# Turning the second unit of each edge turn by DMA in the first column group of a windowed-attention backward kernel

## The chip, the cores and the metric

The kernel runs on one core of a Trainium2 chip. The metric is the device time of one execution in microseconds (us); lower is better. TensorE is PE in the profile, with its weight loads as PEld; VectorE is DVE, ScalarE is ACT, GpSimd is POOL, SyncE is SP. SP computes nothing here: it issues DMAs, in order, and waits in order.

## The reference, cut to what matters

A layer mixes sliding-window attention `a` and a gated feed-forward block `b` by a sigmoid gate `g`; the kernel returns the output and the gradients of all inputs and weights.

```python
qkv = (x @ wqkv).reshape(B, S, 3, H, Dh)             # S=2048, D=512, H=32, Dh=16
scores = einsum("bhqd,bhkd->bhqk", q, k) * Dh**-0.5
mask = (i - j >= 0) & (i - j < 256)                  # a window of 256 keys
p = softmax(where(mask, scores, -1e9));  a = (p @ v) @ wo
gate = x @ W_gate;  up = x @ W_up
b = (relu(gate) * up) @ W_down
g = sigmoid((x * gate_w).sum(-1));  out = g * a + (1 - g) * b
# and the vector-Jacobian product of out with grad_out, for x, wqkv, wo, W_gate, W_up, W_down, gate_w
```

## The kernel before, in words

There are three stages. The feed-forward stage, with its gradients, runs to about 257 us of the profiled span, the attention stage from there to about 713 us, and the last stage, which sums `out` and `dx`, to the end.

The attention stage works on four column groups `c` of 128 columns (8 heads each) and, within a group, on sixteen query blocks of 128 rows. The window lets a query block `q` see the key blocks `q`, `q-1` and `q-2`. The work is cut into *turns*: 46 in each column group, six for every two query blocks. A turn has two *units* (`x` = 0 and 1), each of two heads and up to two (query, key) blocks. Turns 0, 1, 3 and 4 of the six are pair turns (the blocks on and next to the diagonal). Turns 2 and 5 are *edge* turns: their blocks are `(k, k-2)`, where the window ends.

What happens to one turn, over the turns that follow it:

- `products` (L667): PE computes the scores S of this turn and, beside them, the products D of the turn before (`dO` times V). S and D have one PSUM buffer each.
- `front` (L700): ACT takes the exponential of S into the tile `PP`, for both units in one instruction. Edge turns use a tile of two buffers of their own, pair turns one of four; either way a buffer comes round again after six turns.
- `mask` (L710): POOL zeroes what lies outside the window. In an edge turn this is one instruction over the whole tile.
- `gradp` (L717), one turn later: DVE multiplies `PP` by D into the second half of `PP`.
- `flip`: the products for `dK` and `dV` need `PP` turned, with its rows on the other axis. Where `u.dma` is set, SP issues one DMA transpose (L763) right behind `gradp`, one turn after the unit's own. Where it isn't, PE turns eight 128x128 blocks (L771) two turns after the unit's own, into a PSUM tile that DVE or ACT then copies out (L74, L72; `share` picks the engine by a planner's running sum of costs). In the kernel before, of a turn with two blocks unit 0 goes by DMA and unit 1 by PE, except in the first two query blocks of group 0 and the last two of group 3, where all goes by PE.
- `rowsum` (L734, L736): PE sums over `PP`; POOL makes `rq` and others of it (L790 to L805).
- `cd_piece` (L492, L495): PE multiplies the turned `PP` by `rq`. A piece waits for its query block's sums plus three turns (`closed[...] + 3 <= turn`), which puts a turned edge unit's first use at least seven turns behind the unit's own.

The whole order is written out by a loop over `turn` under a manual schedule, so each engine has its instructions in a fixed order. Into the turns it also puts the projections of the next group (L146, L172: a DMA transpose of query and `dO` rows on SP, once in twelve turns), the stores of finished rows (`spill`, L506 on SP, 512 KB each), loads of turned weights (L523 on SP), and in groups 1 to 3 the weight gradients of the group before (L600, L603), whose inputs are loaded at L573.

The lines that decide how a unit is turned:

```python
u.edge = blocks[-1][1] == blocks[-1][0] - 2
u.dma = x == 0 and len(blocks) == 2 and (c > 0 or q > 0) and (c < DC - 1 or q < NT - 2)
u.turn = u.at + (1 if u.dma else 2)
```

Of the kernel before, what the change touches and what calls it, by code (L numbers as in the profile page):

```python
# [22 lines left out]
def kernel(  # L23
# [31 lines left out]
    NT = S // P  # L55
    DC = D // P
# [410 lines left out]
    if True:  # L467
# [166 lines left out]
        for c in range(DC):  # L634
            def pair_of(q):
                return [(q, q), (q + 1, q)]

            def edges_of(r):
                return [(k, k - 2) for k in (r, r + 1) if 2 <= k < NT]

            for q in range(0, NT, 2):
                if q + 2 < NT:
                    its = ((pair_of(q), 0), (pair_of(q), 2), (edges_of(q + 1), 0), (pair_of(q + 1), 2), (pair_of(q + 1), 0),
                           (edges_of(q + 2), 2))
                else:
                    its = ((pair_of(q), 0), (pair_of(q), 2), ([(q + 1, q + 1), (q + 1, q - 1)], 0), ([(q + 1, q + 1)], 2))
                for k, (blocks, g) in enumerate(its):
                    two = []
                    for x in range(2):
                        u = Unit()  # L650
                        u.c, u.q, u.g, u.x, u.blocks, u.nb, u.at = c, q + k // 3, g + x, x, blocks, len(blocks), len(turns_)
                        u.edge = blocks[-1][1] == blocks[-1][0] - 2
                        u.dma = x == 0 and len(blocks) == 2 and (c > 0 or q > 0) and (c < DC - 1 or q < NT - 2)
                        u.turn = u.at + (1 if u.dma else 2)
                        two.append(u)
                    turns_.append(two)
# [218 lines left out]
        with tc.manual_schedule():  # L875
# [49 lines left out]
            while turn < NI + 3 or ev or cdq or bg or sums:  # L925
# [9 lines left out]
                if us and (turn == 0 or turns_[turn - 1][0].q != us[0].q):  # L935
                    c, j = us[0].c, us[0].q
# [215 lines left out]
```

## Time and profile before

| | us |
|---|---|
| median of 3 runs | 911.15 (909.12 to 911.76) |
| the profiled execution | 905.92 |
| span in its profile | 904.2 |
| granted clock, mean over the span | 0.992 |
| first column group, first L700 to first L700 of the next group | 258.0 to 361.0 |
| groups 1 and 2, in the same way | 114.1, 115.1 |

The profiled execution took 1.7 us more than its span, and lies 5.2 us below the median of the timed runs. Times within the span are counted from its start. A busy share is the time in which an engine had an instruction, not the time in which it could not have taken another; SP's busy time is not counted on the page and is read from its timeline.

### The profile page before, as it was taken

The page shows a single profiled execution, that of the slowest core. Times are in us where ns is not written, and L with a number is a line of the kernel's source. Part 1 is how long each engine was busy: PE and PEld are TensorE (multiplying, and loading weights), DVE is VectorE, ACT ScalarE, POOL GpSimd, SP SyncE. Part 2 cuts the span into 40 slices and gives each one's busy share as a digit, 9 for nine tenths or more (in the row PEclk, how much of TensorE's full clock was granted, in tenths as well). Part 3 has the DMA queues.
Part 4 walks back from the last instruction along what each step waited for, and adds up shares of the span by engine and source line. Part 5 has one row for each costly group of instructions (what it writes and reads, how often), then busy time and mean ns, then how long its engine had stood idle before and what let it go on. Part 6 is the DMA issues. An engine that isn't in the chain of part 4 may idle for free. (4 is left out here: it accounts for less than half of the span.)

```text
span 904.2 us, 29627 instructions
## 1 busy us (share of the span) xinstructions
PE 865.2 (96%) x12569; PEld 563.4 (62%) x12569; DVE 492.8 (55%) x754; ACT 389.9 (43%) x565; POOL 474.5 (52%) x883
## 2 busy tenths in 40 slices
PE   7999999999988999999999999999899999999998
PEld 4566555565657777777777767777577744444443
DVE  4543322233247888878778777788677322322322
ACT  5522222223247676666557655667464311111111
POOL 2544444454327777976668766687566512222221
PEclk9999999999989999999999999999899999999999
DMA  9989899988726999999978999999999996777750
GB/s 282 210 182 228 214 209 201 225 202 199 191 56 96 149 148 170 146 152 217 181 113 140 132 238 161 135 164 173 219 178 216 248 278 155 187 196 193 195 124 27
DMA packets 444334, 161.25 MB, mean 178 GB/s; under 512 B 362696, under 2 KB 441896, under 8 KB 444200
## 3 DMA queue, kind: packets, MB, share of 16 engines
q1 hardware_dynamic: 418520, 133.13, 81.7%
q10 hardware_dynamic: 23856, 20.98, 8.2%
q0 software_dynamic: 1824, 5.25, 1.7%
q8 instruction: 98, 1.61, 0.7%
q14 instruction: 36, 0.29, 0.1%
HBM read 38.44 MB, written 38.41 MB: 85 GB/s over the span
## 5 line engine op out<-in xcount | busy, mean ns | idle before, releaser
L717 DVE TENSOR_TENSOR PP<-PP,D 128x1024 bf16<-128x1024 bf16 (+1 forms) x184 | 219.5, 1193 | 69.4 <-POOL PP L710 24.9
L700 ACT ACTIVATE PP<-S 128x1024 bf16<-128x1024 f32 (+1 forms) x184 | 185.2, 1006 | 96.3 <-PE D L667 48.2
L710 POOL TENSOR_SCALAR_AFFINE_SELECT PP<-PP 128x512 bf16<-128x512 bf16 (+1 forms) x188 | 143.5, 764 | 108.8 <-ACT PP L700 93.4
L74 DVE COPY p<-pt 128x1024 bf16<-128x1024 bf16 x167 | 114.3, 684 | 16.5 <-PE pt L771 16.3
L771 PE MATMUL pt<-ident,PP 128*128 128x128 bf16 x1536 | 117.9, 221 | 1.7 <-DVE p L74 0.9
L350 POOL TENSOR_TENSOR hT<-rg,upm 128x512 bf16<-128x512 bf16 x44 | 52.4, 1192 | 126.1 <-DVE upm L348 105.4
L734 PE MATMUL BA<-KV,PP 128*128 128x33 bf16 x1440 | 106.6, 180 | 6.1 <-ACT BAs L72 6.1
L383 PE MATMUL wps<-dgu_r,x_r 128*128 128x256 bf16 x704 | 105.6, 272 | 3.7 <-DVE wst L74 3.4
L734 PEld LDWEIGHTS <-PP 128*128 128x128 bf16 x1440 | 85.6, 96 | 31.2 <-issue 11.2
L736 PE MATMUL BA<-KV,PP 128*128 128x17 bf16 x1440 | 102.2, 170 | 0.3 <-issue 0.3
L492 PE MATMUL CD<-rq,p 128*128 128x32 bf16 x1440 | 95.0, 176 | 0.0
L495 PE MATMUL CD<-rq,p 128*128 128x16 bf16 x1440 | 93.8, 169 | 1.1 <-issue 1.1
L736 PEld LDWEIGHTS <-PP 128*128 128x128 bf16 x1440 | 84.7, 96 | 13.5 <-issue 8.6
L383 PEld LDWEIGHTS <-x_r 128*128 128x128 bf16 x704 | 68.8, 98 | 35.7 <-issue 5.4
L771 PEld LDWEIGHTS <-PP 128*128 128x128 bf16 x1536 | 89.5, 98 | 2.0 <-issue 2.0
L667 PE MATMUL S<-zT,K 32*128 32x128 bf16 (+3 forms) x1056 | 78.4, 241 | 5.4 <-ACT PP L700 2.7
L495 PEld LDWEIGHTS <-p 128*128 128x128 bf16 x1440 | 80.6, 96 | 1.5 <-issue 1.2
L492 PEld LDWEIGHTS <-p 128*128 128x128 bf16 x1440 | 80.8, 96 | 0.3
L667 PE MATMUL D<-zT,V 32*128 32x128 bf16 (+3 forms) x1056 | 73.3, 239 | 4.1 <-DVE PP L717 3.6
L1072 ACT COPY a_sb<-aps 128x512 f32<-128x512 f32 x16 | 9.4, 586 | 145.9 <-issue 133.0
L348 DVE SCALAR_TENSOR_TENSOR upm<-rg,ups 128x512 bf16<-128x512 bf16 x44 | 30.2, 686 | 68.5 <-PE ups L336 43.8
L385 PE MATMUL dps<-db_r,h_r 128*128 128x512 bf16 x176 | 66.7, 379 | 0.0
(144 smaller groups left out, 1471.4 us busy)
## 6 DMA issues: line engine op xcount, KB each, us to landing
dqkvo_d<-rows_st SPq DMA_DIRECT2D x14, 512.0 KB, 4.7
hT_d<-hT ACTq DMA_DIRECT2D x44, 128.0 KB, 2.5
dgT_d<-dgu ACTq DMA_DIRECT2D x44, 128.0 KB, 2.9
duT_d<-dgu ACTq DMA_DIRECT2D x44, 128.0 KB, 2.8
duT_g<-duT_d SPq DMA_DIRECT2D x8, 640.0 KB, 5.3
dgT_g<-dgT_d SPq DMA_DIRECT2D x7, 640.0 KB, 8.0
gt<-hT_d SPq DMA_DIRECT2D x7, 640.0 KB, 5.8
dar<-da_d SPq DMA_DIRECT2D x16, 256.0 KB, 4.6
```

The costliest lines, as they stand in the source:

```text
L74: nc.vector.tensor_copy(out, in_)
L383: nc.tensor.matmul(acc["w"][:, c, :], lhsT=x_r[:, t, c * P:(c + 1) * P], rhs=k.dgu_r[:, :, i, :], start=(go_ and c % 2 == 0), stop=no_, sk ...
L385: nc.tensor.matmul(acc["d"][:], lhsT=k.h_r[:, i, :], rhs=db_r[:, t, :], start=go_, stop=no_)
L492: nc.tensor.matmul(cd[0][:, h, :], lhsT=p2[:, 0, pr, :], rhs=rq[:, h, 0:2 * Dh], start=cd[1], stop=True, skip_group_check=True)
L495: nc.tensor.matmul(cd[0][:, h, 0:Dh], lhsT=p2[:, 1, pr, :], rhs=rq[:, h, 2 * Dh:3 * Dh], start=False, stop=True, skip_group_check=True)
L667: nc.tensor.matmul(dst, lhsT=proj[(u.c, kb // TPG)][nm + ("", "1")[par]][rows[par], (kb % TPG) * P:(kb % TPG + 1) * P], rhs=proj[(u.c, qb ...
L700: nc.scalar.activation(two[:].rearrange("p x a b q -> p x a (b q)")[:, :, 0, 0:n], flat(us[0].S[:], n), ACT.Exp)
L710: nc.gpsimd.affine_select(out=out, in_=out, compare_op=ALU.is_ge, fill=0.0, base=0 if up else -1, pattern=[[0, 2], [0, b1 - b0], [1 if up ...
L717: nc.vector.tensor_tensor(out=v(1), in0=v(0), in1=flat(vs[0].D[:], n), op=ALU.mult)
L734: nc.tensor.matmul(BA[:, h, 0:33], lhsT=u.PP[:, 0, 2 * i + pr, :], rhs=kv[:, kb % TPG, h, 1:34], start=(first and pr == 0), stop=True, ski ...
L736: nc.tensor.matmul(BA[:, h, 33:50], lhsT=u.PP[:, 1, 2 * i + pr, :], rhs=kv[:, kb % TPG, h, 0:17], start=False, stop=True, skip_group_check ...
L771: nc.tensor.transpose(pt[:, a, b if u.nb == 2 else 2 * u.x + b, :], u.PP[:, a, b, :], ident[:])
```

## The change

In column group 0, unit 1 of an edge turn with two blocks now also has `u.dma` set. So its `flip` is moved from two turns behind the unit to one turn behind it, and issues a DMA transpose on SP, directly behind that of unit 0, in the place of eight PE transposes and a copy out of PSUM. Thirteen units are concerned: two edge turns for each two query blocks from block 2 to block 13, and one for the last two. Nothing is changed for pair turns, for query blocks 0 and 1, or for the groups 1 to 3. As there are fewer copies to share out, `share` gives a few others to another engine: on the whole DVE has eight copies of turned units and two of `KV` fewer, ACT five copies of turned units fewer and two of `KV` more.

```diff
                         u.edge = blocks[-1][1] == blocks[-1][0] - 2
-                        u.dma = x == 0 and len(blocks) == 2 and (c > 0 or q > 0) and (c < DC - 1 or q < NT - 2)
+                        u.dma = (x == 0 or c == 0 and u.edge) and len(blocks) == 2 and (c > 0 or q > 0) and (c < DC - 1 or q < NT - 2)
                         u.turn = u.at + (1 if u.dma else 2)
```

## The prediction

> **What bounds the stage.** I read the windows first, cut to the stretch of group 0 in which turns go by DMA, then the groups of instructions of that stretch, then the timelines of PE, DVE and SP.
>
> ```profile
> 277.00:361.00 84.00, 81.11 (x2030) 64.10 (x2028) 73.77 (x106) 59.99 (x78) 66.88 (x150) 1.00 1.02 150
> ```
> ```profile
> L717 DVE TENSOR_TENSOR PP<-PP,D 128x1024 bf16<-128x1024 bf16 x39 | 47.2, 1211 | 8.4 <-POOL PP L710 7.5
> ...
> L771 PE MATMUL pt<-ident,PP 128*128 128x128 bf16 x312 | 23.7, 218 | 0.0
> L74 DVE COPY p<-pt 128x1024 bf16<-128x1024 bf16 x33 | 22.6, 684 | 0.5 <-PE pt L771 0.3
> ```
>
> The columns of the window are its length, then the busy time of PE, PEld, DVE, ACT and POOL, the clock, the DMA share and GB/s. PE is busy for 81.1 of 84 us and DVE for 73.8, at full clock. The turns repeat: three of them (two pair, one edge) take about 6.5 us (the L700 at 317.44, 318.94, 321.26 and 323.93 begin one such round). PE's timeline there is closed to within a tenth of a us at the scores of a turn. So PE bounds the stage, with DVE just behind it. SP's timeline shows the third resource:
>
> ```profile
> 336.83 3.45 SPq L763 DMA_TRANSPOSE p<-PP  x2
> 340.33 1.96 SPq L172 DMA_TRANSPOSE rows<-zT  x1
> 342.39 1.25 SPq L523 DMA_TRANSPOSE p<-in_A_wqkv_dram  x1
> 343.73 2.69 SPq L763 DMA_TRANSPOSE p<-PP  x2
> 346.48 1.72 SPq L523 DMA_TRANSPOSE p<-in_A_wqkv_dram  x1
> 348.28 9.68 SPq L763 DMA_TRANSPOSE p<-PP  x6
> ```
>
> These are issues with hardly a gap: for 21 us SP was behind, in the kernel before already.
>
> **What is taken off PE, DVE and ACT.** Each of the 13 units loses eight transposes:
>
> ```profile
> 322.35 0.46 PEld L771 LDWEIGHTS <-PP 128*128 128x128 bf16 x8
> 322.77 0.10 PEld L146 LDWEIGHTS <-p 128*128 128x128 bf16 x1
> ```
>
> The next work begins 0.42 to 0.44 us behind the first of them, so PE loses 13 x 0.44 = 5.7 us. DVE loses 8 copies of 0.684 and two of KV of 0.53, together 6.5 us; ACT loses 5 of 1.01 and gains two of 0.59, together 3.9 us off. Not all of the 5.7 would show. The flip removed stands in the third turn of a round. There DVE's L717 runs from 321.83 to 323.00, and the next products need D free. They began at 323.35, so a turn without the flip could start them at 323.0: 0.35 us gained. 13 x 0.35 = 4.6 us is the gain if nothing else is late; the ends are 0 (where the odd half of K or V stands ahead of L717 on DVE, as at 328.35) and 5.7.
>
> **What is added on SP.** 13 transposes, each directly behind its unit 0's. They wait for the same L717, so this wait is nothing new; what is new is SP's time:
>
> ```profile
> L763 SPq DMA_TRANSPOSE p<-PP x39: 1231/1302/2273, 277.3 to 361.3; - x39
> ...
> DMA to landing us min/median/max: 3.0/4.2/5.8
> ```
>
> An issue takes 1.23 us when SP is idle. With a queue it takes more: from 338.81 to 357.96 twelve transposes follow each other in 19.15 us, 1.60 each. Issues of 1.3 alternate with some of about 2.0. The long ones (340.33, 346.48, 351.03, 355.90) fall together with packets of the instruction queue:
>
> ```profile
> q8 instruction: 15, 0.25, 1.1%
> ```
>
> Fifteen of these, one in some 5.4 us, of 0.9 to 1.3 us each; during one, hardly a packet of a transpose is moved. Now the sum for SP, from the first round that is changed (issue at 282.30) to the end of group 0's last issue (362.70), 80.4 us. Before: 37 of L763, 4 of L172, 2 of L523, 43 transposes, and two stores (L506, 0.38 and 1.50 us). At 1.60 that is 68.8 + 1.9 = 70.7 us: it fits. After: 56 transposes, 89.6 + 1.9 = 91.5 us. It doesn't fit, by 11.1 us, even if the rest ran no faster than before. In a round of two query blocks (13.05 us) that is 8.5 transposes, 13.6 us, where 6.5 took 10.4.
>
> **Who waits.** A transpose reads `PP`, and L700 writes that buffer again six turns later; in the compiled order L700 waits for a DMA semaphore as well as for DVE and PE, in edge turns of the changed kernel for two. How late may SP be? An edge turn of before:
>
> ```profile
> 317.44 1.02 ACT L700 ACTIVATE PP<-S 128x1024 bf16<-128x1024 f32 x1
> ...
> 330.44 1.03 ACT L700 ACTIVATE PP<-S 128x1024 bf16<-128x1024 f32 x1
> ```
>
> Its transpose was issued at 320.90, with no lag, and landed 3.84 later, at 324.74; the buffer was wanted at 330.44. So 5.7 us were left. Over group 0 the sum of lag and margin is mostly 4.5 to 5.7; I take 5.0. In the busy stretch above, where lag was up to 3.7 us, only 1.1 of it was left: before, nothing waited, but it was near. Once it is used up, ACT waits in L700, with the copies of BA, K, V and zT (L72, L88) queued behind it, and PE for S at the next L667. The first use of a turned unit, seven turns on, comes later than this and so isn't what binds.
>
> **The sum.** 11.1 us too much SP work, less 5.0 that lag may take up, less about 1 that the first turns of group 1 give back (four transposes in five turns, with gaps of 2.0 and 2.8 us on SP): 5 us later than before at the end of the stage. The 4.6 us won on PE isn't subtracted: it only makes SP's queue begin to bind earlier. The chain behind the stage is PE's, and so 5 us go to the end. On the profile's own 905.9 that is 910.9; on the median, 5.2 higher, 911.15 + 5.0 = 916.1. I choose 1.60 because it is measured in this stage, with this traffic, at the first place where SP is behind. The other rows: 1.23 to 1.30 between instruction packets below, and above it this one of group 1, behind four loads of 256 KB:
>
> ```profile
> 376.83 11.09 SPq L763 DMA_TRANSPOSE p<-PP  x6
> ```
>
> which is 1.85 each.
>
> A figure from elsewhere would give another answer. The Trainium skill, in "DMA: Bandwidth & Descriptors", section "Latency and other measured facts", has an effective 261 GB/s for a DMA transpose: 256 KB in 1.0 us (an estimate from it), 58 us of work in the 80.4, and nothing would be late. The trace doesn't agree: 262 KB in 1.60 us is 164 GB/s. Against the change speaks a rule of the Trainium skill, in "VectorE: DVE Perf Modes", section "Rules for kernel authors": 128x128 on TensorE where PSUM will do, by DMA otherwise; it gives no price, and the trace has none for it but the queue above.
>
> **Rivals.**
>
> *SP is hidden, the kernel is faster.* If a queue were served at 1.33 us (1.29 and a gap, as between instruction packets), the work would be 56 x 1.33 + 1.9 = 76.4 us, in a stretch of 80.4 - 4.6 = 75.8; lag takes up the 0.6 that is over. Then 4.6 us are won: 911.15 - 4.6 = 906.6, at best 905.4. For it: two of three issues do take 1.3, and no L700 waits for a DMA before. Against it: the instruction packets come with PE's work and don't go away. The change turns from loss to gain where the SP work is (80.4 + 6.0 - 1.9) / 56 = 1.51 us each. Chance 0.23.
>
> *It comes out even.* From 343.73 to 351.03, five transposes take 7.30 us, 1.46 each; nine to 357.96 take 1.58. Between, at 1.52, 85.1 + 1.9 - 80.4 - 6.0 = 0.6 us: 911.8. Chance 0.20.
>
> *The queue does more harm than its own length.* At 1.72, between the two measured ends of a full queue, 96.3 + 1.9 - 80.4 - 6.0 = 11.8 us, 923: lag that is carried into group 1 meets its loads (L573) and stores, where 8 us to landing were seen. For it: the stores' transfers slow their neighbours (2.11 and 1.59 us at 310). Chance 0.12.
>
> That the change doesn't do what it says is ruled out: in the compiled order SP has 13 pairs of L763, and PE 104 transposes less.
>
> **Numbers.** The forecast (915 to 919) has 0.45, the harm case 0.12, even 0.20, faster 0.23. A run of this kernel can tell about 0.3% (2.7 us) from no change. That gives 0.23 faster, 0.20 same, 0.57 slower. The range runs from the faster case, nearly at its best, to just below the harm case's middle: 906.0 to 922.0. The likelier sign's own range is 914 to 923.
>
> **What would show it.** Right: in SP's timeline from about 300 on no gaps between issues, at 1.5 to 1.7 us each; in the waits, ACT's L700 on a DMA `p<-PP`, which before never shows, for 5 to 10 us in all, most of it past 335, where the stores and L523 come; PE's share in 277 to 361 below 0.93; group 0 at 106 to 109 us instead of 102.9, groups 1 and 2 at their 114 and 115. Wrong: SP keeping gaps of half a us in most rounds, no DMA in L700's waits, and rounds of 12.4 us instead of 13.05; then the cost per transpose is what failed. If L700 waits but the stage is no longer, the 5 us of margin were too few. Wrong in another way: if PE waits at L492 for a landing, or if the loss stands in groups 1 to 3.

## The result and the profile after

The changed kernel takes 917.6 us (median of 14 runs, 910.32 to 924.89), the kernel before, run between them, 910.99 (14 runs, 907.69 to 916.74). The ratio is 1.0075, with a 95% interval of 1.0049 to 1.0101: slower by 6.6 us, where 5.0 were forecast. A second measurement (run `after_again`, below) gives 1.0084. The first profile of the changed kernel fell on an execution in a slower state (924.89 us), so the lines below are from `after_again`, whose profiled execution took 916.87 us with a span of 915.2.

The window over the part of group 0 that the prediction read first (length, then busy time of PE, PEld, DVE, ACT and POOL, granted clock, DMA share, GB/s):

```profile
277.00:361.00 84.00, 75.85 (x1800) 57.14 (x1800) 65.22 (x91) 52.82 (x69) 62.35 (x140) 0.90 1.11 165
```

Every engine has got emptier: PE from 81.1 us to 75.9, DVE from 73.8 to 65.2. Only the DMA share went up, from 1.02 to 1.11. The granted clock fell from 1.00 to 0.90.

The groups of instructions of this stretch (window 277 to 369; busy time and mean ns, then idle time ahead and what ended it):

```profile
L717 DVE TENSOR_TENSOR PP<-PP,D 128x1024 bf16<-128x1024 bf16 x39 | 47.4, 1216 | 17.2 <-POOL PP L710 10.9 <-PE D L667 4.4 <-PE S L667 0.7
L700 ACT ACTIVATE PP<-S 128x1024 bf16<-128x1024 f32 (+1 forms) x40 | 40.5, 1012 | 26.7 <-PE D L667 12.4 <-DMA p<-PP 8.5 <-PE S L667 3.7
L771 PE MATMUL pt<-ident,PP 128*128 128x128 bf16 x224 | 18.5, 231 | 0.0
L74 DVE COPY p<-pt 128x1024 bf16<-128x1024 bf16 x26 | 17.8, 683 | 0.2
```

L717 costs what it cost, but now stands idle for 17.2 us where it was 8.4. L700 has a releaser that it didn't have before, `DMA p<-PP`: the transpose that still reads the buffer which L700 wants to write. SP's timeline (start, duration, issues):

```profile
291.09 22.23 SPq L763 DMA_TRANSPOSE p<-PP  x14
...
320.56 22.57 SPq L763 DMA_TRANSPOSE p<-PP  x14
...
343.86 3.57 SPq L763 DMA_TRANSPOSE p<-PP  x2
347.48 1.95 SPq L172 DMA_TRANSPOSE rows<-zT  x1
349.52 1.25 SPq L523 DMA_TRANSPOSE p<-in_A_wqkv_dram  x1
350.87 4.93 SPq L763 DMA_TRANSPOSE p<-PP  x3
355.85 1.29 SPq L523 DMA_TRANSPOSE p<-in_A_wqkv_dram  x1
357.24 12.60 SPq L763 DMA_TRANSPOSE p<-PP  x9
```

Fourteen issues in 22.23 us are 1.59 each, fourteen in 22.57 are 1.61. The longest gap between two issues from 283.25 to 377.67 us is 0.42 us: SP works through the whole of the changed part without a break.

### The profile page after: what moved, and what is told of

It is laid out like the page before. It is cut to its first block, busy times and chain, and to the rows that moved or that the text cites. A ratio compares the mean times of both kernels' runs of the same rounds, so it can differ in the third digit from the quotient of the medians.

```text
span 923.2 us, 29309 instructions
## 1 busy us (share of the span) xinstructions
PE 857.5 (93%) x12335; PEld 562.8 (61%) x12465; DVE 488.4 (53%) x744; ACT 386.2 (42%) x562; POOL 474.2 (51%) x883
## 3 DMA queue, kind: packets, MB, share of 16 engines
q8 instruction: 97, 1.59, 0.8%
## 5 line engine op out<-in xcount | busy, mean ns | idle before, releaser
L717 DVE TENSOR_TENSOR PP<-PP,D 128x1024 bf16<-128x1024 bf16 (+1 forms) x184 | 219.7, 1194 | 83.4 <-POOL PP L710 28.2
L700 ACT ACTIVATE PP<-S 128x1024 bf16<-128x1024 f32 (+1 forms) x184 | 185.1, 1006 | 119.4 <-PE D L667 57.0
L74 DVE COPY p<-pt 128x1024 bf16<-128x1024 bf16 x159 | 108.9, 685 | 15.3 <-PE pt L771 14.9
L771 PE MATMUL pt<-ident,PP 128*128 128x128 bf16 x1432 | 113.0, 225 | 1.0 <-DVE p L74 0.9
L495 PE MATMUL CD<-rq,p 128*128 128x16 bf16 x1440 | 94.1, 170 | 1.9 <-issue 1.9
L492 PE MATMUL CD<-rq,p 128*128 128x32 bf16 x1440 | 95.5, 177 | 0.3 <-DMA p<-PP 0.3
L667 PE MATMUL S<-zT,K 32*128 32x128 bf16 (+3 forms) x1056 | 80.5, 245 | 12.7 <-ACT PP L700 7.7
L495 PEld LDWEIGHTS <-p 128*128 128x128 bf16 x1440 | 81.0, 96 | 2.3 <-issue 2.0
L492 PEld LDWEIGHTS <-p 128*128 128x128 bf16 x1440 | 81.2, 96 | 0.7 <-DMA p<-PP 0.4
L667 PEld LDWEIGHTS <-K 16*128 16x128 bf16 (+1 forms) x1056 | 35.3, 94 | 51.4 <-issue 44.0
```

What stands on the lines that cost most here:

```text
L74: nc.vector.tensor_copy(out, in_)
L492: nc.tensor.matmul(cd[0][:, h, :], lhsT=p2[:, 0, pr, :], rhs=rq[:, h, 0:2 * Dh], start=cd[1], stop=True, skip_group_check=True)
L495: nc.tensor.matmul(cd[0][:, h, 0:Dh], lhsT=p2[:, 1, pr, :], rhs=rq[:, h, 2 * Dh:3 * Dh], start=False, stop=True, skip_group_check=True)
L667: nc.tensor.matmul(dst, lhsT=proj[(u.c, kb // TPG)][nm + ("", "1")[par]][rows[par], (kb % TPG) * P:(kb % TPG + 1) * P], rhs=proj[(u.c, qb ...
L700: nc.scalar.activation(two[:].rearrange("p x a b q -> p x a (b q)")[:, :, 0, 0:n], flat(us[0].S[:], n), ACT.Exp)
L717: nc.vector.tensor_tensor(out=v(1), in0=v(0), in1=flat(vs[0].D[:], n), op=ALU.mult)
```

## The experiments

All ratios are to the kernel before, measured on the same chip in the same session, with 95% intervals. Diffs are against the changed kernel unless they say "before".

The theory: the DMA transposes are served one after the other; with thirteen more the queue is longer than the stage, and `PP` buffers come free too late. The first rival says that the queue is harmless and something else about the thirteen units costs the time. The second says that PE's relief is real and only partly covered by the queue's loss, so that without it the loss would be 11 to 12 us. A third says that the time goes in stretches at half clock.

**The changed kernel once more** (`after_again`, no edit).

> The changed kernel once more, for a profile at full clock. Queue theory: the transposes of group 0 stand in one queue on SP, served at about 1.6 us each; once its lag has used up the six turns after which a PP buffer comes round, L700 waits. Then group 0 is 5 to 9 us longer than before, SP has no gaps from about 285 to 375, L700 waits for p<-PP by 5 to 12 us, and groups 1 and 2 are at 114 to 115. Total 5 to 8 us over before. Clock rival: the loss comes from stretches at half clock that follow pauses of PE. Then a profile at full clock shows group 0 no longer than 104 us.

Measured: 918.78 us, 1.0084 (1.0052 to 1.0116). The profile confirms the queue, but it isn't at full clock (0.979 over the span), so it doesn't decide against the clock. Nor do the timed runs: their median granted clock is 0.978, that of the kernel before in the same session 0.989, which over 916 us is some 10 us of full clock lost.

**The DMA without the relief** (`e_both`, from before). The thirteen units are turned on PE as before, and a DMA transpose of the same data goes into a tile that nobody reads.

```diff
+u.twice = c == 0 and u.edge and x == 1 and len(blocks) == 2 and q > 0
...
+elif v.twice:
+    spare = gwp.tile([P, 2, D], BF, tag="dar", bufs=4, name="spare")[:].rearrange("p a (b q) -> p (a b) q", q=P)
+    nc.sync.dma_start_transpose(out=spare, in_=v.PP.rearrange("p a b q -> p (a b) q"))
```

> The 13 units are turned on PE as before, and a DMA transpose of each is issued as well, into a spare tile that nobody reads; SP has the work of the changed kernel, PE, DVE and ACT that of before. Queue theory: PE's relief is worth nothing while the queue binds, so the time is that of the changed kernel within 1.5 us (5 to 8 us over before). Rival, a plain sum of the work taken off PE and a fixed price of each DMA: the 4.6 us of PE's relief are lost on top, 11 to 12 us over before.

Measured: 917.88 us, 1.0074 (1.0042 to 1.0105), the same as the changed kernel. In the waits of ACT (us in all, times, longest) the same exponential stands as L701:

```profile
ACT PP L701 <- DMA spare<-PP: 6.7, 2, 3.7
ACT PP L701 <- DMA p<-PP: 3.9, 2, 2.3
```

So the added DMAs by themselves bring a loss of this size, and the rival's 11 to 12 us are out. On balance, taking 104 transposes off PE and 8 copies off DVE is worth nothing as long as these DMAs are there. Whether that is because the queue alone sets the time is not shown: the median granted clock of these runs is 0.987, near that of the kernel before (0.989), where the changed kernel has 0.978. So `e_both` loses its 6.5 us with PE at almost the old clock, and the changed kernel with less work on PE at a lower clock; the relief may be lost to the clock as well as to the queue (see `e_fill`).

**The relief without the DMA** (`e_skip`, from before). The thirteen units are not turned at all; their products are made with unit 0's turned data in their place, so the output is not the reference's.

```diff
+u.skip = c == 0 and u.edge and x == 1 and len(blocks) == 2 and q > 0
-p2 = wides[u.at][:, u.x if u.nb == 2 else 0, :, :, :]
+p2 = wides[u.at][:, u.x if u.nb == 2 and not u.skip else 0, :, :, :]
+if u.skip:
+    return
```

> The 13 units are not turned at all (the output lacks their part of the key and value gradients: unit 0's turned data stand in for unit 1's); SP has the work of before, PE, DVE and ACT that of the changed kernel. Queue theory and the first part of the sum: 4.6 us faster than before (0 to 5.7), 0.995 of it. If PE's relief is worth nothing even without the queue, the same as before.

Measured: 907.28 us, 0.9957 (0.9936 to 0.9978), 4.1 us faster than before, and no exponential waits for a DMA. That is what the relief would bring if the DMA were free. Its one profile is of its slowest run (910.88 us) and has half clock too: three stretches between 275.5 and 313.0, 20.4 us in all, without a wait for a DMA, and a group 0 of 105.0 us. So not every half clock comes from the queue.

**Seven units instead of thirteen** (`e_k2`): of each two query blocks only the first edge turn.

```diff
-(x == 0 or c == 0 and u.edge)
+(x == 0 or c == 0 and u.edge and k == 2)
```

> Only the first edge turn of each six is changed, 7 units instead of 13. Queue theory: 50 transposes of 1.6 us and 1.9 of stores are 81.9 us in 80.4, and lag can take up 5, so hardly anything waits; 7 x 0.35 = 2.4 us of PE's relief are won, less about 1 for the bunch at the weight loads: 0 to 2.4 us faster than before. Rival, a fixed price of each transpose (6.6 us / 13 = 0.5 us): 3.5 us slower than before.

Measured: 909.83 us, 0.9984 (0.9963 to 1.0005). Seven of the thirteen transposes do not cost half the loss but none of it. The fixed price, 3.5 us slower, is outside the interval; a threshold fits. In the profile L700 still waited for a DMA in three turns, 3.5 us in all (here and below in the window 277 to 385, where the changed kernel has 10.8).

**Both units in one DMA** (`e_one`): the number of transposes is that of before, the bytes are those of the changed kernel.

```diff
+if vs and all(v.dma for v in vs):
+    for v in vs:
+        place(v)
+    nc.sync.dma_start_transpose(out=wides[vs[0].at][:].rearrange("p x a b q -> p (x a b) q"),
+                                in_=vs[0].two[:].rearrange("p x a b q -> p (x a b) q"))
```

> As the changed kernel, but the two units of such an edge turn are turned by one DMA transpose of 512 KB instead of two of 256 KB. If the queue's price goes by bytes (blocks that the DMA engines turn), one of these takes some 3.2 us of SP and the time stays at 5 to 8 us over before. If it goes by issue, 13 issues fall away, SP's work is that of before, and the time is that of the version that doesn't turn these units: about 4 us faster than before.

Measured: 916.29 us, 1.0037 (1.0015 to 1.0058). The large ones, by the view of that line (minimum, median and maximum ns):

```profile
L972 SPq DMA_TRANSPOSE p<-PP x13: 1844/2968/3229, 284.2 to 370.9; - x13
```

In this one profile (of an execution of 922.62 us) a transpose of 512 KB takes 2.97 us at the median, nearly twice the 1.6 of one with 256 KB. So the price goes mostly with the bytes; a fixed price per transpose would have made the kernel some 4 us faster than before. Thirteen of 2.97 us are 38.6 us of SP where twenty-six of 1.6 are 41.6. The loss is 3.4 us by the ratio instead of 6.6 to 7.4, but the intervals overlap, so that a saving is likely and not shown; L700 still waits for a DMA, 7.9 us in three turns.

**More `PP` buffers** (`e_ring`): in group 0 edge turns have four buffers instead of two and pair turns six instead of four; the added ones lie in a store buffer (`rows_st`) that isn't used yet.

```diff
+own, more = (2, 2) if edge else (4, 2)
+if us[0].c == 0:
...
+    i = ring.get(edge, 0)
+    ring[edge] = (i + 1) % (own + more)
+if i >= own:
+    k0 = (i - own + (0 if edge else 2)) * 16 * P
+    two = ring["tile"][:, k0:k0 + 16 * P].rearrange("p (x a b q) -> p x a b q", x=2, a=2, b=4)
```

> As the changed kernel, but in group 0 edge turns have four PP buffers instead of two and pair turns six instead of four (the added ones lie in the second rows_st buffer, which group 0 doesn't need): a buffer comes round after 12 and 9 turns instead of 6. Queue theory: L700's wait for p<-PP, 10.8 us in the changed kernel, goes to below 3 us in group 0; part of it comes back as PE waiting at L492 for a landing (first use is seven turns on, and a lag of 10 us with 4.5 to landing comes to that), and as lag that group 1 starts with. 0 to 5 us over before, so 2 to 6 us better than the changed kernel. If L700's wait were not what costs, the time stays at that of the changed kernel.

Measured: 919.62 us, 1.0073 (1.0047 to 1.0098): no better, which the theory as it stood did not expect. The waits of this kernel, window 277 to 385:

```profile
POOL rq L804 <- DMA rows<-zT: 5.3, 3, 4.7
PEld L492 <- DMA p<-ring: 2.1, 2, 1.5
PE CD L492 <- DMA p<-ring: 1.9, 2, 1.4
```

The exponential's wait on `p<-PP` is gone from group 0, but the time isn't. The turned rows (the transpose of L172) stand in the same queue and come late in their turn, as do the turned units for PE itself. The longest of these waits, 4.7 us of POOL, holds up the mask behind it, DVE's product behind the mask, and PE for 4.63 us up to 354.21. Here the queue found another waiter when the first was given room.

**Two loads moved out of the stage** (`e_late`): the two L523 transposes of `wqkv` at turns around 345 us are put into group 1.

```diff
-plan = {3: turns("wqkv", A_wqkv, 0, 4, "p0"), 7: turns("wqkv", A_wqkv, 4, 8, "p1"),
+plan = {7: turns("wqkv", A_wqkv, 0, 4, "p0") + turns("wqkv", A_wqkv, 4, 8, "p1"),
```

> As the changed kernel, but the two turned loads of wqkv (L523) that stand in group 0 at the queue's worst place are issued in group 1 instead. Queue theory: 2 x 1.6 = 3.2 us less SP work in group 0, and as L700 waits there, 3 us less of its waits: 2 to 5 us over before. If the loss were a fixed price of each of the 13 transposes, nothing changes: 5 to 8 us over before.

Measured: 915.93 us, 1.0042 (1.0017 to 1.0067). Two transposes fewer, 3.2 us of queue, and the loss is 3.7 us instead of 6.6 to 7.4; the intervals overlap, so this is a hint in the expected direction. L700's waits for a DMA fell only from 10.8 to 9.3 us, in five turns, where 3 us less were expected. The same edit made to the kernel before (`b_late`) is its control:

> The kernel before with only the two turned loads of wqkv moved from group 0 to group 1: a control for the other two. Queue theory: before, nothing waits for the queue in group 0, so the same as before within 0.2%. If group 0's bunch did cost before, 1 to 2 us faster.

Measured: 911.75 us, 1.0001 (0.9975 to 1.0026). In the kernel before, moving the loads is worth nothing that the measurement can tell.

**Four units** (`e_q4`): only query blocks 2 to 5, long before the stores and the loads.

```diff
-(x == 0 or c == 0 and u.edge)
+(x == 0 or c == 0 and u.edge and q < 6)
```

> Only the edge turns of the first two rounds (query blocks 2 to 5) are changed, 4 units, where SP still had gaps of about 1 us in each turn. Queue theory: no L700 waits for a DMA before 320 us of the span, lag there stays under 4 us, and 4 x 0.35 = 1.4 us are won: 0 to 2 us faster than before. A fixed price of 0.5 us for each: 2 us slower.

Measured: 910.68 us, 0.9980 (0.9963 to 0.9997), with no wait of L700 for a DMA. It has the lowest ratio of the versions that compute everything: 1.6 to 1.8 us better than the kernel before, which is hardly more than the measurement can tell, and its interval overlaps that of `e_k2`.

**Both ways to shorten the queue** (`e_late_k2`): seven units, and the two loads moved.

> Both reliefs of the queue together: the first edge turn of each six alone is changed (7 units), and the two turned loads of wqkv are issued in group 1. Queue theory: 48 transposes of 1.6 us and 1.9 are 78.7 us in 80.4, no bunch is left, lag stays under 4 us, L700 waits for no p<-PP in group 0, and all of 7 x 0.35 = 2.4 us is won: 2 to 3 us faster than before. A fixed price of each transpose: 3.5 us slower.

Measured: 911.36 us, 0.9994 (0.9971 to 1.0017). No L700 waited for a DMA in the profile, and yet the 2 to 3 us did not come. Why is open; the interval reaches from 2.6 us faster to 1.5 us slower.

**Work put into PE's pause** (`e_fill`): 22 matmuls without use, some 2.4 us, in turn 39, into a PSUM half that nobody reads.

```diff
+if turn == 39:
+    for _ in range(22):
+        nc.tensor.matmul(CDs["spare"], lhsT=ident[:], rhs=x_r[:, 0, 0:2 * P], start=False, stop=True, skip_group_check=True)
```

> As the changed kernel, but in turn 39 PE gets 22 matmuls into an unused half of a PSUM bank (about 2.4 us that nobody reads), just where it stood still for 2.5 us in the changed kernel's profile because L700 waited for a landing; there 10.2 us at half the granted clock followed. If that pause brings the half clock, and it costs: no half clock at 350 to 362, and 2 to 4 us better than the changed kernel. If the queue alone sets the time, within 1.5 us of the changed kernel either way. If PE doesn't stand still there, 2.4 us worse.

What it is for shows in three windows of `after_again` around the wait at 349 us:

```profile
345.00:349.00 4.00, 4.00 (x86) 2.79 (x85) 3.02 (x4) 1.51 (x2) 3.47 (x7) 1.00 1.36 182
349.00:351.50 2.50, 0.19 (x4) 0.05 (x3) 1.25 (x4) 1.51 (x3) 0.42 (x1) 1.00 0.87 188
351.50:362.00 10.50, 9.91 (x192) 6.99 (x192) 6.24 (x9) 5.67 (x9) 6.63 (x18) 0.51 1.18 183
```

PE stands for 2.31 us, from 349.13 to 351.45, and over the next 10.5 us its granted clock is 0.51. The chain in between, from the timelines of ACT and PE: L700 waits 3.17 us for the landing of a transpose, the copy of BA is queued behind it, and PE's row sums wait for that copy.

```profile
349.99 1.02 ACT L700 ACTIVATE PP<-S 128x1024 bf16<-128x1024 f32 x1 [3.17 <-DMA p<-PP]
350.91 0.49 ACT L72 COPY BAs<-BA 128x400 f32<-128x400 f32 x1
```
```profile
351.45 0.18 PE L734 MATMUL BA<-KV,PP 128*128 128x33 bf16 x1 [2.31 <-ACT BAs L72]
```

The same windows in `e_fill`:

```profile
345.00:349.00 4.00, 4.00 (x105) 2.82 (x101) 3.02 (x4) 2.58 (x4) 3.56 (x8) 1.00 1.66 193
349.00:351.50 2.50, 2.02 (x25) 1.52 (x22) 2.14 (x4) 1.47 (x3) 1.82 (x5) 1.00 0.66 135
351.50:362.00 10.50, 9.34 (x220) 7.27 (x218) 6.44 (x8) 5.78 (x8) 5.84 (x15) 0.93 1.18 199
```

The pause is filled, the clock stays at 0.93, and the window has 220 matmul records instead of 192. Measured: 914.16 us, 1.0027 (1.0006 to 1.0047). Added work made the changed kernel some 4 to 5 us faster; the interval lies just below both of the changed kernel's. The transposes are all still there, so the queue's length alone does not set the time: the branch of the expectation with 1.5 us either way is out. The median granted clock of the timed runs is 0.985, against 0.978 in `after_again`. Its one profile has group 0 no shorter (109.5 us against 109.6), since L700 still waits 4.1 us and another half-clock stretch of 6.8 us stands at 323, and shows the gain in group 1 (113.3 against 118.2). So that 4 to 5 us went is measured; that they went only through this one stretch is not shown.

**Group 1's share** (`e_spill`): in the profiles of the changed kernel group 1 is 4 us longer too. There PE stands 1.9 us at L495, and a half-clock stretch of 6.8 us follows. The profile names nothing that L495 waited for; the transposes issued beside two L506 stores landed some 8 us after their issue, at about that time, and are the suspects. The two stores are issued at query block 8 instead of 6.

```diff
-if j == 6 and c > 0:
+if j == (8 if c == 1 else 6) and c > 0:
```

> As the changed kernel, but in group 1 the two stores (L506) of group 0's last rows are issued four and more turns later (query block 8 instead of 6). In two profiles of the changed kernel PE stood still twice near 425 us, in turn 70, at L495 and L734, for 2.1 and 1.3 to 1.6 us, behind transposes that landed 8 us after issue beside these stores; a half clock of 6.8 us followed, and group 1 was 4 us longer than before. If that is the second part of the loss: group 1 at 113 to 115 us, no half clock there, and 3 to 4 us better than the changed kernel, 2 to 4 us over before. If the loss is all in group 0, no better than the changed kernel.

Measured: 918.61 us, 1.0087 (1.0055 to 1.0119). In its profile group 1 is back at 115.0 us without the half clock, group 0 is at 112.2, and the time is no better. So taking the stall out of group 1 did not make the kernel faster here; how much of the 6.6 us lies there stays open.

## Why the prediction was right

**The queue's length.** The step that decided, 56 transposes at 1.60 and two stores, 91.5 us where 80.4 were to be had, held to the half us: in `after_again` these issues run from 283.25 to 374.41, 91.2 us. None of its L763 took less than 1.23 us, and the rate that the Trainium skill gives in "DMA: Bandwidth & Descriptors", section "Latency and other measured facts", would have made it 1.0 (an estimate from 261 GB/s); the trace's own rate under load decides. The reading of the instruction packets was off, though the measured 1.60 doesn't rest on it: during the one of 0.89 us at 346.65, in the profile of before, some 400 packets of the queue that carries the transposes began, and 28 in the 0.8 us behind it.

**Who waits.** As said: ACT's L700 on `p<-PP`, which before never showed. Most of it is late (window 277 to 385: us in all, times, longest):

```profile
ACT PP L700 <- DMA p<-PP: 10.8, 4, 3.4
```

Of the 10.8 us, 8.9 lie past 335, the last 2.3 of them at the first turns of group 1. Between 5 and 10 were forecast, so this is a little more. PE's share in 277 to 361 is 75.85 / 84 = 0.90 (below 0.93, as said). In group 0 PE did not wait at L492 for a landing.

**PE's 4.6 us, not subtracted.** Both sizes are shown: 4.1 us where nothing takes their place (`e_skip`), nothing on balance where the thirteen DMAs are there (`e_both`). The reason that was given, that the relief only makes the queue bind earlier, is not shown by itself: the changed kernel's lower clock could have taken the relief as well.

**The terms that were mis-sized.** 11.1 less 5.0 of margin less 1 made 5; 6.6 were measured. The sum let an engine that waits lose its wait and no more, and has no term for the clock. But the waits that stopped PE for some 2 us or more were followed by stretches at half clock, and with one such pause filled `e_fill` is 4 to 5 us faster and loses 3. So the queue's overhang less its slack does not alone make the 6.6, and that 5.0 came so near is in part luck: a term for the clock is missing, and the terms taken off would then be too small. The two of them, margin and give-back, no run measures by themselves. SP's queue was full from 283 on, not from about 300, and the first of the four waits, 1.9 us, ends at 320.82, before the place where most was expected. Group 0 took 109.6 us in this profile, just past the 106 to 109 forecast, and group 1 118.2 instead of its 114; that the loss might stand in a later group was named as a way of being wrong, and for some part of it this is so in the profiles. Profiles of one execution say little on such parts: group 0 is 109.6 here, 113.7 in `e_both` and 107.2 in `e_ring`, at the same total within the intervals.

**The rivals.** That SP is hidden is out by its timeline and by `e_both`. Its turning point, 1.51 us per transpose or, in other terms, a queue some 5 us shorter, fits: with six or nine units fewer (`e_k2`, `e_q4`) the sign is no longer a loss. The case that comes out even and the one that loses 12 us lie outside the interval.

## What to carry to other kernels

Before moving work to a queue, add up the queue: issues times the duration of one under this load, against the time between the first and the last of them; an idle-looking engine can hold a full queue, and what is over minus the slack of the buffers is a first estimate of the loss (5 us against 6.6 here). More buffers did not help a queue that was too long in itself (`e_ring`), since the next waiter was in the same queue; fewer items did, and a part of a change can be worth having where the whole isn't (`e_q4`). Count a stall of TensorE by what its clock does afterwards too.

## What the runs showed of the hardware

- The half clock: the pause of PE from 349.13 to 351.45 was followed by 10.2 us at a granted clock of 0.5; other pauses of about 2 us, by 3.4 or 6.8 us. Shorter ones went both ways: 1.19 us ending at 257.6 in the profile of before and 1.01 us ending at 322.3 in `after_again` had half clock within 2 us behind them, 1.13 us ending at 708.6 in before had none. And in `e_skip` the stretches that begin at 289.1 (10.2 us) and 309.6 (3.4 us) had no pause of PE above 0.8 us in the 13 us ahead of them, so one long pause is not needed. The profile of before has two half-clock stretches in its whole span, that of `after_again` seven. The Trainium skill, in "TensorE: Matmul & The Clock Gate", section "Why this matters for your kernels", sets the limit at gaps of some 3 us; here 2.3 and less were enough.
- 22 matmuls that compute nothing, put into a pause of PE, made a kernel faster by about 0.5% (`e_fill`).
- The price of a transpose from SBUF to SBUF goes by bytes: 256 KB took 1.6 us in a full queue, 512 KB 2.97.
